# The second exchange of a spectral layer: half of it copied block by block inside SBUF

## The chip, the cores and the metric

The kernel runs on one core of a Trainium2 chip. The metric is the device time of one launch in microseconds (us). TensorE is called PE, VectorE DVE, ScalarE ACT, GpSimd POOL, SyncE SP; the last issues most DMAs. SBUF is the on-chip memory with 128 partitions, PSUM the accumulators' memory, DRAM the memory outside.

## The reference

Four layers on one sequence of 2048 rows by 512 columns, in bfloat16: spectral, attention, spectral, attention, each added to its input. Both kinds start with a layer norm. The spectral layer is a two-dimensional real FFT, a product with a complex weight, and the inverse:

```python
def _A_ref(x, w_r, w_i):
    B, S, D = x.shape
    X = rfft2(x.astype(float32), axes=(-2, -1))
    W = w_r + 1j * w_i
    X = X * W
    return irfft2(X, s=(S, D), axes=(-2, -1)).astype(bfloat16)

x = x + _A_ref(_layernorm(x), A_w_r, A_w_i)
x = x + _B_ref(_layernorm(x), B_wq, B_wk, B_wv, B_wo)
x = x + _A_ref(_layernorm(x), A_w_r, A_w_i)
x = x + _B_ref(_layernorm(x), B_wq, B_wk, B_wv, B_wo)
```

`_B_ref` is attention with 32 query heads of 16 and one shared key and value head. It takes most of the time and is not touched by the change.

## The kernel before, in words

The spectral layer does each FFT as matrix products. The FFT along the 2048 rows is split as 2048 = 128 x 16: a product over 128 points, a twiddle, and a product over 16 points follow one another, and between the products the data must be dealt out anew over the partitions. That is an *exchange*. There are two in a layer: one on the way forward (tiles A1 to A2, through DRAM tensor D1) and one on the way back (tiles B1 to B2, through D2). The 256 complex frequencies along the columns are worked in two halves, `h` = 0 and 1, of 128 each; a tile such as B1 has the shape 128 partitions x 2 halves x 16 blocks x 256 numbers.

The steps around the change are these, by the names in `spectral_layer`:

- `blocks(q)` (L261): POOL builds the block tables H1, H2, H2N and for two of the four `q` H1N, from a table HC and a mask: fourteen products a layer (L266). In the second layer they stand on POOL ahead of the last `ln_rstd` (L163) of the norm, on which the forward product waits.
- `filtered(j)` (L330), j = 0 to 7, four for each half: the 16-point product of four blocks (PE, table G), a copy to X (ACT, L339) and the products with the weights (DVE, L343, L345), for odd j the sums into Z in `joined` (L358, L359).
- `back(j)` (L361): the 16-point inverse of the four blocks `b4` to `b4 + 3`, two blocks at a time: PE products with the H tables, then a copy from PSUM to B1 (L375 on ACT; L373 on DVE for the last pair of all), then one DMA on SP that writes the two blocks to D2 (L376).
- `cross2(h, g, eng)` (L378): one of four reads of D2 to B2 for a half. Each takes four of the 16 values of `t` for all 128 partitions, and needs all sixteen blocks of the half to be in D2. For half 0 all four are on SP; for half 1 two are on SP and two on ACT (L421).
- `along(q, h)` (L396): for two values of `t`, four PE products with lhsT from B2 and the table CS (L401), then a copy to AT on ACT or DVE (L404, L406).
- `last(t, h)` (L410): the product along the columns into a PSUM sum, started with the residual (L414 to L416), after which ACT copies the row tile to x_sb (L435) and DVE takes its statistics (L157).

The order of `filtered`, `back` and the reads of half 0 is written out by hand:

```python
STEPS = "f0 f1 f2 b0 f3 b1 b2 j f4 b3 x0 f5 f6 b4 f7 b5 j7 b6 b7"
```

Here `f` is `filtered`, `b` is `back`, `j` is `joined`, `x0` is the four reads of half 0. So half 0's reads go out behind the last write of b3, while steps 4 to 7 (half 1) are still to be computed. After the steps come the eight `along` of half 0, the four reads of half 1, `weights(20)` (in the first layer: loads of wq and wo on SP), four `last(t, 0)`, and then the loop of `along(q, 1)` and `last`. PE, ACT, DVE and SP run in the order in which the program names the instructions; POOL's order is left to the scheduler. DMAs take their completion semaphores from eight in turn, and a DMA waits for the one that used its semaphore before.

In the partition index m of B1 the value m = 8 t + a belongs to `t` of 16 and `a` of 8, since H's columns stand in that order; in B2 the partition index is 16 a + b, with b the block.

Of the kernel before, what the change touches and what calls it, by code (L numbers as in the profile page):

```python
# [10 lines left out]
ALU = mybir.AluOpType  # L11
P = 128
BF = mybir.dt.bfloat16
# [4 lines left out]
S, D, H, DH = 2048, 512, 32, 16  # L18
# [28 lines left out]
LASTW = 6  # L47
NEGATE = 7
DIRECT = (0, 2, 4, 6)
STEPS = "f0 f1 f2 b0 f3 b1 b2 j f4 b3 x0 f5 f6 b4 f7 b5 j7 b6 b7"  # L50
NORMED, NORMG = (1,), ((3,), (3,), (3,))
OUTK, LATE_AT = 2, 4
TWICE = ((7,), 8)
# [23 lines left out]
def host_tables():  # L77
    import ml_dtypes
    bf = lambda a: np.ascontiguousarray(np.asarray(a, dtype=np.float32).astype(ml_dtypes.bfloat16))
    tabs = {}  # L80
    p = np.arange(P, dtype=np.float64)
    m = np.arange(P, dtype=np.float64)
    t16 = np.arange(16, dtype=np.float64)

    row = (128 * np.arange(4)[None, :, None] + np.arange(P)[:, None, None]).astype(np.float64)
    ff = (np.arange(256)[None, None, :] + 1).astype(np.float64)

    half = 2 * np.pi * np.arange(256) / 512.0
    cos, sin = np.cos(half), np.sin(half)
    cos[128], sin[0] = 0.0, 0.0  # L90
    cos[129:], sin[129:] = -cos[1:128][::-1], sin[1:128][::-1]
    turn = (row * ff).astype(np.int64) % 512
    c, s = np.concatenate([cos, -cos])[turn], -np.concatenate([sin, -sin])[turn]
    tabs["PH"] = bf(np.concatenate([c[..., :128], s[..., :128], c[..., 128:], s[..., 128:]], axis=2))

    ang = 2 * np.pi * (16 * p[:, None, None] + t16[None, :, None]) * m[None, None, :] / 2048.0
    tabs["C1"], tabs["S1"] = bf(np.cos(ang)), bf(np.sin(ang))

    ti, ai = np.divmod(np.arange(P), 8)
    same = (ai[:, None] == ai[None, :]).astype(np.float64)  # L100
    ang = 2 * np.pi * ti[:, None] * ti[None, :] / 16.0
    tabs["G"] = bf(np.stack([same * np.cos(ang), same * np.sin(ang), -same * np.sin(ang)], axis=1))

    b16 = np.arange(16, dtype=np.float64)
    mm = 16 * ai[:, None, None] + b16[None, :, None]
    ang = 2 * np.pi * (ti[:, None, None] * t16[None, None, :] / 16.0 + t16[None, None, :] * mm / 2048.0)
    tabs["HC"] = bf(np.stack([np.cos(ang), np.sin(ang), -np.sin(ang), -np.cos(ang)], axis=1))
    tabs["mask8"] = bf(ai[:, None] == np.arange(8)[None, :])

    ang = 2 * np.pi * m[:, None] * p[None, :] / 128.0  # L110
    tabs["CS"] = bf(np.stack([np.concatenate([np.cos(ang), np.sin(ang)], axis=1),
                              np.concatenate([-np.sin(ang), np.cos(ang)], axis=1)], axis=1))

    frow = (128 * np.arange(2)[None, :, None] + np.arange(P)[:, None, None] + 1).astype(np.float64)
    dd = np.arange(512)[None, None, :].astype(np.float64)
    ang = 2 * np.pi * frow * dd / 512.0
    cf = np.where(frow == 256, 1.0, 2.0) / (S * D)
    tabs["PSC"] = bf(cf * np.cos(ang))
    tabs["PSS"] = bf(-cf * np.sin(ang))
    tabs["ident"] = bf(np.eye(P, dtype=np.float32))  # L120
    tabs["hmask"] = (np.arange(P)[:, None] // DH % 2 == np.arange(2)[None, :]).astype(np.float32)
    return tabs


class Tables:


    def __init__(self, nc):
        self.nc, self.host, self.dram = nc, host_tables(), {}
# [82 lines left out]
def rotate(nc, ps, c, s, sn, re_im, first, begin=True, end=True):  # L212

    nc.tensor.matmul(ps, lhsT=c, rhs=re_im, start=begin, stop=False, skip_group_check=True)  # L214
    nc.tensor.matmul(ps[:, 0:128], lhsT=s, rhs=re_im[:, 128:256], start=False, stop=False, skip_group_check=True)
    nc.tensor.matmul(ps[:, 128:256], lhsT=sn, rhs=re_im[:, 0:128], start=False, stop=end, skip_group_check=True)  # L216


def spectral_layer(nc, tc, tabs, ht, A_w_r, A_w_i, x_sb, bigp, pre, norm, att, feed, weights):
    C1, S1, S1N, PH, ident = (tabs[n] for n in ("C1", "S1", "S1N", "PH", "ident"))  # L220
    with tc.tile_pool(name="workA", bufs=2) as work, tc.tile_pool(name="tabA", bufs=1) as tabA, \
# [31 lines left out]
            weights(k)  # L253

        D1 = dram.tile([2, 16, P, 256], BF, name="D1")
        D2 = dram.tile([2, P, 16, 256], BF, name="D2")
        turned = len(feed.xT)
        xT = feed.xT[0] if turned else bigp.tile([P, NC, 16, P], BF, name="xT", tag="big")
        Pk, A1, A2 = big("Pk"), big("A1"), big("A2")
# [1 line left out]
        def blocks(q):  # L261

            b = slice(4 * q, 4 * q + 4)
            shape = [P, 4, 16, 8]
            for i, H in enumerate([H1[:, b], H2[:, b], H2N[:, b]] + ([H1N[q]] if q in H1N else [])):
                nc.gpsimd.tensor_tensor(out=H.rearrange("p b (t a) -> p b t a", a=8),  # L266
                                        in0=tabs["HC"][:, i, b].unsqueeze(3).to_broadcast(shape),
                                        in1=tabs["mask8"].unsqueeze(1).unsqueeze(1).to_broadcast(shape), op=ALU.mult)

        def forward(k, h):  # L270

# [26 lines left out]
        for k in range(9 + behind):  # L298
# [6 lines left out]
            at = k - behind  # L305
# [21 lines left out]
        Z, B1, B2 = big("Z"), big("B1"), big("B2")  # L327
        M = big("M").rearrange("p h t c -> p (h t c)").rearrange("p (i j b r f) -> p i j b r f", i=2, j=4, b=4, r=2)

        def filtered(j):  # L330

            h, b4 = j // 4, 4 * (j % 4)
            hf = slice(128 * h, 128 * h + 128)
            X = work.tile([P, 4, 2, 128], BF, name="X", tag="X", bufs=3)
            for b in range(b4, b4 + 4, 2):
                ps = bank()
                for i in range(2):
                    rotate(nc, ps[:, i, :], G[:, 0, :], G[:, 1, :], G[:, 2, :], A2[:, h, b + i, :], i == 0)
                nc.scalar.copy(out=X[:, b - b4:b - b4 + 2, :, :], in_=ps.rearrange("p j (r f) -> p j r f", r=2))  # L339
            m1, m2 = (M[:, i, j % 4] for i in range(2))  # L340
            wrb = wr_sb[:, b4:b4 + 4, hf].unsqueeze(2).to_broadcast([P, 4, 2, 128])
            wib = wi_sb[:, b4:b4 + 4, hf].unsqueeze(2).to_broadcast([P, 4, 2, 128])
            nc.vector.tensor_tensor(out=m1, in0=X, in1=wrb, op=ALU.mult)  # L343
            joined()
            nc.vector.tensor_tensor(out=m2, in0=X, in1=wib, op=ALU.mult)  # L345
            if j in DIRECT:
                unsummed[j] = (m1, m2)
            else:
                products.append((j, m1, m2))
# [3 lines left out]
        def joined():  # L353

            while products:
                j, m1, m2 = products.pop()
                Zv = Z[:, j // 4, 4 * (j % 4):4 * (j % 4) + 4, :].rearrange("p b (r f) -> p b r f", r=2)
                nc.vector.tensor_tensor(out=Zv[:, :, 0, :], in0=m1[:, :, 0, :], in1=m2[:, :, 1, :], op=ALU.subtract)  # L358
                nc.vector.tensor_tensor(out=Zv[:, :, 1, :], in0=m1[:, :, 1, :], in1=m2[:, :, 0, :], op=ALU.add)  # L359

        def back(j):  # L361
            h, b4 = j // 4, 4 * (j % 4)
            for b in range(b4, b4 + 4, 2):
                ps = bank()
                for i in range(2):
                    if j in DIRECT:
                        m1, m2 = (m[:, b + i - b4].rearrange("p r f -> p (r f)") for m in unsummed[j])
                        rotate(nc, ps[:, i, :], H1[:, b + i, :], H2N[:, b + i, :], H2[:, b + i, :], m1, i == 0, True, False)
                        rotate(nc, ps[:, i, :], H2N[:, b + i, :], H1N[j % 4][:, b + i - b4, :], H1[:, b + i, :], m2, False, False)
                    else:  # L370
                        rotate(nc, ps[:, i, :], H1[:, b + i, :], H2N[:, b + i, :], H2[:, b + i, :], Z[:, h, b + i, :], i == 0)
                if j == 7 and b > b4:
                    nc.vector.tensor_copy(out=B1[:, h, b:b + 2, :], in_=ps)  # L373
                else:
                    nc.scalar.copy(out=B1[:, h, b:b + 2, :], in_=ps)  # L375
                nc.sync.dma_start(out=D2[h, :, b:b + 2, :], in_=B1[:, h, b:b + 2, :])  # L376

        def cross2(h, g, eng):  # L378
            eng.dma_start(out=B2[:, h, 4 * g:4 * g + 4, :],
                          in_=D2[h].rearrange("(t a) b c -> t (a b) c", t=16)[4 * g:4 * g + 4].rearrange("t m c -> m t c"))  # L380

        for step in STEPS.split():
            j = int(step[1:] or 0)
            if step[0] == "f":
                filtered(j)
            elif step[0] == "b":
                back(j)
            elif step[0] == "j":
                joined()
            else:  # L390
                for g in range(4):
                    cross2(0, g, nc.sync)

        AT = big("AT").rearrange("p h t c -> p (h t c)").rearrange("p (t h c) -> p t h c", t=16, h=2)

# [21 lines left out]

        for q in range(8):
            along(q, 0, q % 2 == 0)
        for g in range(4):  # L420
            cross2(1, g, (nc.sync, nc.scalar)[g % 2])  # L421
        weights(20)
        early = 4
        for t in range(early):
# [2 lines left out]
        for q in range(9):  # L427
# [9 lines left out]
            g, odd = divmod(q - 3, 2)  # L437
# [863 lines left out]
```

## Time and profile before

| what | value |
|---|---|
| median of 3 runs | 1403.78 us (1402.68 to 1403.95) |
| the profiled execution's own time | 1402.49 us |
| its span, from the first to the last instruction | 1400.7 us |
| PE busy | 1348.2 us (96%) |
| ACT busy | 1331.4 us (95%) |
| DVE busy | 1305.8 us (93%) |
| POOL busy | 849.4 us (61%) |
| DMA moved | 32.70 MB |
| D<-B writes, 128 KB each | 32, median 3.0 us from issue to landing |
| B<-D reads, 256 KB each | 12 on SP, 3.9 us; 4 on ACT, 4.4 us |

The profile is of one execution. A row "A<-D" is a DMA or an instruction that writes tile A from tile D; tile names come without numbers, so A is A1 or A2, D is D1 or D2, B is B1 or B2. "SPq" is SP's queue of DMA issues. The first spectral layer lies in the first 80 us of the span, the second between about 705 and 790 us; the rest is attention, in which ACT, PE and DVE are all nearly full. The high shares of the whole page are those of attention. The change lies in the spectral layers, so they are read by themselves.

### The profile page before, as it was taken

To read this page: it belongs to the slowest core of one execution; us is meant where nothing else is said; L and a number is where in the kernel's file an instruction comes from. 1 tells how busy PE (TensorE), PEld (TensorE's weight loads), DVE (VectorE), ACT (ScalarE), POOL (GpSimd) and SP (SyncE) were. 2 spreads that over 40 slices of the span, in tenths; PEclk is the share of its full clock that TensorE was granted. 3 is DMA by queue.
4 is the path that set the end of the run, shared out by engine and by line. 5 is a ranking of instruction groups with operands and counts; after the bars stand their busy time and mean duration, and the time that the engine had idled before them with its cause. 6 is when DMAs were issued, how large, how long until landed. Compare 5 with 4: busy or idle time off the path is not lost.

```text
span 1400.7 us, 35023 instructions
## 1 busy us (share of the span) xinstructions
PE 1348.2 (96%) x14146; PEld 477.7 (34%) x14214; DVE 1305.8 (93%) x2253; ACT 1331.4 (95%) x1542; POOL 849.4 (61%) x507
## 2 busy tenths in 40 slices
PE   7899999999999999999999999999999999999998
PEld 6752232222222222222277422322223222222222
DVE  5689999999999999999966899999999999999997
ACT  6679999999999999999957899999999999999997
POOL 3325666667666667666640367666667667666664
PEclk9999999999999999999999999999999999999999
DMA  8700000000000000002064000000000000000000
GB/s 243 209 17 2 1 2 2 2 2 2 2 1 1 2 2 2 2 1 37 11 166 137 2 2 2 2 1 9 5 6 2 6 9 5 2 6 5 9 2 16
DMA packets 45395, 32.70 MB, mean 23 GB/s; under 512 B 10160, under 2 KB 43184, under 8 KB 44720
## 3 DMA queue, kind: packets, MB, share of 16 engines
q1 hardware_dynamic: 42832, 29.24, 7.4%
q8 instruction: 111, 1.82, 0.5%
q10 hardware_dynamic: 2400, 1.21, 0.3%
q14 instruction: 52, 0.43, 0.1%
HBM read 18.39 MB, written 10.49 MB: 21 GB/s over the span
## 4 chain that ended last, share of the span: by engine, by line
ACT 48%; PE 33%; issue 9%; DVE 6%; DMA 2%; POOL 1%; SPq 0%; DVEq 0%; ACTq 0%; POOLq 0%
ACT e L1099 47%; PE pv L888 13%; PE sc L933 10%; DVE ph L973 3%; PE aux L933 2%; PE ps L214 1%; PE ps L275 1%; DVE ln_stats L157 1%; PE aux L472 1%; DMA B<-D 1%; DVE ph L1005 1%; PE pv L903 1%; PE aux L701 1%; POOL tab_H L266 1%; PE ps L216 1%
## 5 line engine op out<-in xcount | busy, mean ns | idle before, releaser
L1099 ACT ACTIVATE e<-sc 128x1024 bf16<-128x1024 f32 x1328 | 1218.1, 1163 | 2.9 <-PE sc L933 2.9
L997 POOL TENSOR_TENSOR ph<-ph,step 128x1024 int32<-128x1024 int32 x404 | 763.3, 1893 | 412.3 <-DVE ph L1005 291.8
L973 DVE TENSOR_SCALAR ph<-aux 128x512 uint16<-128x512 f32 x1440 | 904.0, 679 | 20.4 <-PE aux L933 15.8
L888 PE MATMUL pv<-ph,vaug 128*32 128x512 bf16 x4320 | 548.8, 386 | 0.6 <-POOL ph L997 0.3
L933 PE MATMUL sc<-QT,Kv 32*128 32x512 bf16 x2656 | 521.9, 380 | 23.2 <-ACT e L1099 15.9
L888 PE MATMUL pv<-e,vaug 128*32 128x512 bf16 x2656 | 484.0, 384 | 0.3 <-ACT e L1099 0.3
L933 PE MATMUL aux<-QT,Kv 32*128 32x512 bf16 x1440 | 456.0, 384 | 1.0 <-DVE ph L973 0.5
L933 PEld LDWEIGHTS <-Kv 32*128 32x128 bf16 x4096 | 183.2, 91 | 525.5 <-issue 517.2
L903 PE MATMUL pv<-wo_sb,zeros 128*32 128x512 bf16 x1200 | 257.9, 383 | 0.0
L888 PEld LDWEIGHTS <-vaug 128*32 128x32 bf16 x6976 | 147.7, 94 | 293.0 <-issue 282.0
L1005 DVE TENSOR_SCALAR ph<-ph 128x2048 uint16<-128x2048 uint16 x316 | 216.6, 685 | 0.5
L163 POOL TENSOR_TENSOR ln_rstd<-ln_veps,mhalf 128x4 f32<-128x4 f32 x16 | 16.5, 1034 | 107.2 <-DVE ln_veps L162 107.1
L157 DVE BATCH_NORM_STATS2 ln_stats<-x_sb 128x6 f32<-128x512 bf16 x64 | 43.5, 679 | 23.3 <-ACT x_sb L435 17.2
L903 PEld LDWEIGHTS <-zeros 128*32 128x32 bf16 x1200 | 60.1, 94 | 1.9 <-issue 0.3
L803 DVE STREAM_TRANSPOSE oT<-pv 128x512 f32<-128x512 f32 x64 | 45.3, 707 | 9.2 <-PE pv L888 9.2
L186 ACT ACTIVATE Pk<-ps,ln_rstd 128x256 bf16<-128x256 f32 x64 | 26.7, 473 | 21.0 <-PE ps L275 16.1
L289 DVE CAST A<-ps 128x512 bf16<-128x512 f32 x28 | 19.2, 689 | 19.8 <-PE ps L216 18.7
L275 PE MATMUL ps<-tab_PH,xT 128*128 128x256 bf16 x256 | 35.6, 288 | 1.7 <-DMA tab_PH<-const_PH 0.8
L472 PE MATMUL aux<-xTa,wq_sb 128*128 128x512 bf16 x90 | 32.6, 385 | 2.8 <-issue 2.4
L825 POOL TENSOR_TENSOR on<-oT,rden 128x512 bf16<-128x512 f32 x30 | 31.7, 1058 | 2.0 <-DVE rden L829 1.8
L701 PE MATMUL aux<-wo_sb,ph 128*128 128x512 bf16 x72 | 26.1, 383 | 3.6 <-issue 2.1
L275 PEld LDWEIGHTS <-xT 128*128 128x128 bf16 x256 | 25.4, 103 | 6.0 <-issue 1.5
(117 smaller groups left out, 715.2 us busy)
## 6 DMA issues: line engine op xcount, KB each, us to landing
D<-A SPq DMA_DIRECT2D x32, 128.0 KB, 2.7
A<-D SPq DMA_DIRECT2D x16, 256.0 KB, 3.3
D<-B SPq DMA_DIRECT2D x32, 128.0 KB, 3.0
B<-D SPq DMA_DIRECT2D x12, 256.0 KB, 3.9
wr_sb<-in_A_w_r_dram SPq DMA_DIRECT2D x2, 1024.0 KB, 7.0
wi_sb<-in_A_w_i_dram SPq DMA_DIRECT2D x2, 1024.0 KB, 8.9
out_dram<-x_sb SPq DMA_DIRECT2D x15, 128.0 KB, 1.7
x_sb<-in_A_x_dram SPq DMA_DIRECT2D x3, 512.0 KB, 8.2
```

What stands on the lines that cost most here:

```text
L157: nc.vector.bn_stats(st, src)
L275: nc.tensor.matmul(ps[:, j, :], lhsT=xT[:, cc, 2 * k + j, :], rhs=PH[:, cc, 256 * h:256 * h + 256], start=(cc == 0), stop=(cc == NC - 1), ...
L472: self.nc.tensor.matmul(ps, lhsT=w(c), rhs=self.xTq[:, c, qc * 512:(qc + 1) * 512], start=(c == 0), stop=(c == NC - 1), skip_group_check=True)
L701: nc.tensor.matmul(ps, lhsT=OTs[qb][:, g4, kk * P:(kk + 1) * P], rhs=wo_sb[:, g4, :], start=first, stop=last, skip_group_check=True)
L803: end = clock.now(clock.FLIP, lambda: nc.vector.transpose(out=oT[:, par].rearrange("p b c -> p (b c)"), in_=pv), clock.last + clock.MM_END)
L888: nc.tensor.matmul(pv_tiles[gi][32 * i:32 * i + 32, :], lhsT=vaug[:, kc, j, :], rhs=es, start=((gi, i) not in started), stop=(left[gi, i] ...
L903: nc.tensor.matmul(pv_tiles[gi][32 * i:32 * i + 32, :], lhsT=att.zeros, rhs=wo_sb[:, 0, :], start=False, stop=False, skip_group_check=True)
L933: nc.tensor.matmul(out, lhsT=Kv[r, par, kc * P:(kc + 1) * P], rhs=QT[r, g, qb * 512:(qb + 1) * 512], start=True, stop=True, skip_group_che ...
L973: end = clock.now(clock.Z, lambda: nc.vector.tensor_scalar(out=z.bitcast(U16), in0=ps, scalar1=SCALE * LOG2E * 128.0, scalar2=127.0 * 128. ...
L997: nc.gpsimd.tensor_tensor(out=copy.bitcast(I32), in0=z.bitcast(I32), in1=step.to_broadcast([P, w // 2]), op=ALU.add)
L1005: nc.vector.tensor_scalar(out=one.bitcast(U16), in0=z.bitcast(U16), scalar1=float(PHASE[1]), scalar2=None, op0=ALU.add)
L1099: nc.scalar.activation(out=e[:, 0:ng * 512], in_=sc[:, 0:ng, :].rearrange("p a b -> p (a b)"), func=ACT.Exp, scale=SCALE)
```

## The change

The four `back` steps of half 1 (j = 4 to 7) no longer write D2. After each pair of blocks, two DMAs on SP copy the blocks straight from B1 to B2, one block per DMA: 128 source partitions of 512 B each go into eight destination partitions of 8 KB each, four partitions apart. So half 1 has sixteen copies of 64 KB and no reads. The four steps of half 0 still write D2 and read it back, but each read now belongs to one `back` step: it takes the four blocks of step g and fills 32 partitions with 8 KB each.

For this the order of partitions is changed on both sides. H's columns, and so the partitions of B1, become m = 16 a + t, so that the sixteen `t` of one `a` stand side by side; B2's partition becomes 32 g + 4 a + b', where b' is the block within step g, and the rows of the table CS are put into that order on the host. The tables H are computed with their two inner axes exchanged. The products on PE keep their number and shapes.

```diff
-STEPS = "f0 f1 f2 b0 f3 b1 b2 j f4 b3 x0 f5 f6 b4 f7 b5 j7 b6 b7"
+STEPS = "f0 f1 f2 b0 f3 b1 b2 j f4 b3 x0 x1 x2 x3 f5 f6 b4 f7 b5 j7 b6 b7"
...
     tabs["CS"] = bf(np.stack([np.concatenate([np.cos(ang), np.sin(ang)], axis=1),
-                              np.concatenate([-np.sin(ang), np.cos(ang)], axis=1)], axis=1))
+                              np.concatenate([-np.sin(ang), np.cos(ang)], axis=1)], axis=1)[16 * (np.arange(P) // 4 % 8) + 4 * (np.arange(P) // 32) + np.arange(P) % 4])
...
-        D2 = dram.tile([2, P, 16, 256], BF, name="D2")
+        D2 = dram.tile([2, 4, 4, P, 256], BF, name="D2")
...
-            shape = [P, 4, 16, 8]
+            shape = [P, 4, 8, 16]
             for i, H in enumerate([H1[:, b], H2[:, b], H2N[:, b]] + ([H1N[q]] if q in H1N else [])):
-                nc.gpsimd.tensor_tensor(out=H.rearrange("p b (t a) -> p b t a", a=8),
-                                        in0=tabs["HC"][:, i, b].unsqueeze(3).to_broadcast(shape),
-                                        in1=tabs["mask8"].unsqueeze(1).unsqueeze(1).to_broadcast(shape), op=ALU.mult)
+                nc.gpsimd.tensor_tensor(out=H.rearrange("p b (a t) -> p b a t", a=8),
+                                        in0=tabs["HC"][:, i, b].unsqueeze(2).to_broadcast(shape),
+                                        in1=tabs["mask8"].unsqueeze(1).unsqueeze(3).to_broadcast(shape), op=ALU.mult)
...
-                nc.sync.dma_start(out=D2[h, :, b:b + 2, :], in_=B1[:, h, b:b + 2, :])
+                if j >= 4:
+                    for bb in (b, b + 1):
+                        at = 32 * (j % 4) + bb - b4
+                        nc.sync.dma_start(out=B2[at:at + 29:4, h, :, :], in_=B1[:, h, bb, :])
+                else:
+                    nc.sync.dma_start(out=D2[h, j % 4, b - b4:b - b4 + 2].rearrange("b p c -> p b c"), in_=B1[:, h, b:b + 2, :])
 
-        def cross2(h, g, eng):
-            eng.dma_start(out=B2[:, h, 4 * g:4 * g + 4, :],
-                          in_=D2[h].rearrange("(t a) b c -> t (a b) c", t=16)[4 * g:4 * g + 4].rearrange("t m c -> m t c"))
+        def cross2(h, g):
+            nc.sync.dma_start(out=B2[32 * g:32 * g + 32, h, :, :],
+                              in_=D2[h, g].rearrange("b (a t) c -> a b (t c)", t=16))
...
             else:
-                for g in range(4):
-                    cross2(0, g, nc.sync)
+                cross2(j // 4, j % 4)
...
         for q in range(8):
             along(q, 0, q % 2 == 0)
-        for g in range(4):
-            cross2(1, g, (nc.sync, nc.scalar)[g % 2])
         weights(20)
```

## The prediction

> **What bounds the kernel now.** I read the page first (span, shares, the chain of work that ended last), then that chain in order of time around the second exchange of each spectral layer, then PE's timeline there, then what the DMA queues move, and POOL's groups.
>
> ```profile
> span 1400.7 us, 35023 instructions
> ACT 48%; PE 33%; issue 9%; DVE 6%; DMA 2%; POOL 1%; SPq 0%; DVEq 0%; ACTq 0%; POOLq 0%
> ```
> DMA holds 2% of the chain: exchanges end last at only a few places. Here is the chain in order of time in the first spectral layer, then in the second (start, length, what):
>
> ```profile
> 60.70 2.93 DMA D<-B
> 63.76 3.35 DMA B<-D
> 67.16 0.62 PE ps L401 x4
> ...
> 752.65 2.99 DMA D<-B
> 755.76 3.32 DMA B<-D
> 759.12 0.62 PE ps L401 x4
> ```
> The last block of the second half is written to DRAM (2.9 us) and read back (3.3 us), and only then does `along` (L401) go on. PE's timeline says how much of these 6.3 us nobody covers (in brackets: idle before, and who ended it):
>
> ```profile
> 67.16 1.05 PE L401 MATMUL ps<-tab_CS,B 128*128 128x256 bf16 x8 [1.43 <-DMA B<-D]
> ...
> 759.12 0.61 PE L401 MATMUL ps<-tab_CS,B 128*128 128x256 bf16 x4 [1.46 <-DMA B<-D]
> ```
> So PE is ready at 65.73 and 757.66, and all that a shorter second exchange can give is 1.43 + 1.46 = 2.89 us, 0.21% of the time. I take 0.2% (2.8 us) as about what a measurement of this kernel tells from no change. Behind the idle time the chain runs through L401, the sums and the statistics on DVE without slack, so a microsecond there is a microsecond of the end.
>
> **The SP queue and the DMA engines.** One line is one run of issues; then stretches of the busy table (last columns: granted clock, DMA share, GB/s) and one queue's share of the stretch 757.90 to 760.40.
>
> ```profile
> 54.55 2.50 SPq L379 DMA_DIRECT2D B<-D  x4
> 57.09 4.01 SPq L376 DMA_DIRECT2D D<-B  x8
> ...
> 755.80:756.80 1.00, 1.00 (x6) 0.47 (x5) 0.01 (x1) 0.00 (x0) 0.00 (x0) 1.00 0.00 0
> 737.75:738.50 0.75, 0.75 (x13) 0.69 (x10) 0.75 (x4) 0.69 (x2) 0.00 (x0) 1.00 0.72 218
> 757.90:760.40 2.50, 1.05 (x8) 0.70 (x8) 0.00 (x0) 0.63 (x2) 0.00 (x0) 1.00 1.16 319
> ...
> q1 hardware_dynamic: 711, 0.35, 49.2%
> ```
> Eight issues fill 4.01 us: 0.50 us each. The read issued at 755.76 moves nothing until 756.80: 1.04 us to the first packet. Reads into 128 partitions (B<-D, 757.90) run at 319 GB/s, a read into 32 partitions (A<-D, 737.75) at 218. In the last line (same 2.5 us stretch) 711 packets of 512 B take 49.2% of 16 engines: 0.492 x 16 x 2500 / 711 = 28 ns a packet.
>
> **The change, part by part.**
>
> *First half (h=0).* Eight D2 writes keep their number and place; their runs fall from 1 KB to 512 B. The nearest row is D<-A, same shape, median 2.7 us to landing against 3.0 for D<-B: nothing. The four reads now land in 32 partitions each, in 8 KB runs, as A<-D does, and the first `along` waits for all four instead of one. SP reaches them where it did: after the last write of b3, issued 52.46 to 52.78 and 744.05 to 744.50, so at about 52.88 and 744.60. With 1.04 us to the first packet, data starts at 53.92 and 745.64. A 256 KB read at A<-D's 218 GB/s takes 1.20 us; four take 4.8 (at least 3.3, at B<-D's rate). They end at 58.72 and 750.44. PE wants them at 59.4 and 751.4 (first L401), so this stays hidden, by 0.4 us in the first layer with a tail of 0.25.
>
> *Second half (h=1): what goes.* Eight writes and four reads per layer, two of the reads on ACT's queue (1.00 us of issue at 63.77; ACT is idle there from 63.32 to 67.80, so its relief is worth nothing), and the write-then-read wait.
>
> *What comes.* Sixteen copies of 64 KB, all on SP, 128 packets of 512 B each into 8 partitions. SP issue: 16 x 0.50 = 8.0 us from about 55.0, instead of 4.0: the last goes out at 62.5 (first layer; the last B1 tile is ready at 60.37). With a first packet 1.04 us later that is 63.5, not yet the limit; at the longest issue among B<-D's rows (0.97 us) it would go out at 69.6. Behind the copies on SP stand the wq and wo loads (landed 70.86 and 72.31, first used at about 81): still early enough. The program has eight DMA semaphores in turn, so the eighth copy waits for the last read to land (about 750.7) and the ninth for the first copy; at 0.50 us an issue this also ends before the data does.
>
> *The data of a copy* is the price no row shows. From below: 64 KB at 319 GB/s, 0.21 us. From above: if the rate shrinks with the destination partitions from 32 to 8, 218/4 = 55 GB/s, 1.2 us. Going from 128 to 32 partitions cost a factor 319/218 = 1.46; another such step gives 149 GB/s, 0.44 us. Eight rows written side by side, 16 packets of 28 ns each, give 0.45 us. I take 0.45. The copies queue behind the four reads: 16 x 0.45 = 7.2 us. First layer: 53.92 + 4.8 + 7.2 + 0.25 (from the last packet to the semaphore, an estimate: under 0.1 to about 0.5 in the rows) = 66.17, against 65.73: PE idles 0.44 + 0.05 instead of 1.43, gain 0.94. Second layer: 745.64 + 4.8 + 7.2 + 0.25 = 757.89, against 757.66: 0.28 instead of 1.46, gain 1.18. Together 2.1 us.
>
> *H tables on POOL.* The same fourteen products a layer, with the repeated operand changed. This matters in the second layer, where they stand in the chain ahead of the normalisation:
>
> ```profile
> L266 POOL TENSOR_TENSOR tab_H1N<-tab_HC,tab_mask 128x512 bf16<-128x512 bf16 x4 | 4.2, 1038 | 0.0
> L825 POOL TENSOR_TENSOR on<-oT,rden 128x512 bf16<-128x512 f32 x30 | 31.7, 1058 | 2.0 <-DVE rden L829 1.8
> ```
> L825 already repeats one operand along its innermost 16 elements, as the new form does, and takes 1058 ns: at most 0.02 us more, over 14 chained products 0.28; nothing excludes as much less. I take 0, because the element count is the same. The reordered CS table and the reordered partitions of B2 leave `along` with the same shapes; PE, DVE and POOL keep their order.
>
> **Sum.** The profiled execution took 1402.49 us (span 1400.7 and 1.8 around it). 1402.49 - 2.1 = 1400.4. The median of the runs, 1403.78, is 1.29 above that execution, so I give 1401.7, 0.15% less.
>
> **Rivals.**
>
> *A, wholly hidden.* If copies take up to 0.42 us, the last lands before PE needs it and the gain is 2.89: 1399.6 against the profiled execution, 1400.9 on the median. For it: packets of both sides spread over 16 engines would give 0.22 us. Against it: the rate already falls from 319 to 218 with fewer partitions. [...]
>
> *B, the other side: the copies become the bound.* Place: the DMA queue between the last read and the last copy. It decides from 16 t = 67.11 - 53.92 - 5.05, t = 0.51 us a copy (0.52 in the second layer): above that the copies land later than today's read, and each further 0.1 us costs 1.6 us a layer. At 0.65 us PE goes on 2.26 and 2.01 us later than now: 1402.49 + 4.3 = 1406.8, 1408.1 on the median; from 0.61 it is over 0.2%. For it: the fall of the rate with fewer partitions, and that no row has both sides in SBUF. Against it: 28 ns packets with eight rows abreast give 0.45. [...]
>
> *C, the first `along` waits.* If four reads take over 5.2 us they delay PE at 59.4, but PE then also needs the copies later; it costs only what it adds to the copies' end, 0.1 to 0.5 us, and is part of the forecast's own spread.
>
> *D, POOL.* The new table form costs 0.2 us a product more: 14 x 0.2 = 2.8, 1404.5 on the median after the gain. No row speaks for so much.
>
> **Chances.** Forecast, partly hidden (0.42 to 0.52 us a copy): 0.42. A: 0.17. B: 0.36, of it 0.26 beyond 0.61 us. D and the unforeseen: 0.05. Faster by over 0.2%: three quarters of A, which lies on the edge, a tenth of the forecast's cases, 0.01 of the rest: 0.18. Slower: 0.26 of B and 0.04 of the rest: 0.30. Within: 0.52. The range runs from A, with 0.7 for the scatter of the runs, 1400.2, to just past B at 0.65, 1408.5; what lies beyond is the far end of 1.2 us a copy (16 x 0.75 us more a layer, 1425 or so) and luck. The likeliest case alone: 1400.9 to 1403.8.
>
> **What would show it.** PE's idle time before the first L401 of the second half: 0.2 to 0.7 us if right, 0 for A, over 1.5 for B. Time between landings of successive copies when queued: 0.45 us. Reads of the first half: about 1.2 us apart, the last landed by 59.2 and 751.0. L266 at 1.04 us. SP at 0.50 us an issue. Wrong would be: copies slower than 0.51 us, SP issues near 1 us, or an idle PE at 59.4 of over half a microsecond.

## The result, and the profile after

| | median | range | runs |
|---|---|---|---|
| before, beside it | 1404.51 us | 1402.68 to 1406.21 | 8 |
| after | 1408.37 us | 1405.83 to 1410.85 | 8 |

The ratio is 1.0029, with an interval of 1.0018 to 1.0041: the change costs 0.29%, about 4 us, where 2.1 us of gain were forecast. The time lies at the upper end of the range, close to the 1408.1 that rival B gave. That agreement is luck: B gave it for copies 0.65 us apart, and for the 0.70 to 0.73 us that were measured B's own sum gives about 1410.

The page of the profile after, its first line and the shares of the chain of work that ended last:

```profile
span 1408.8 us, 35032 instructions
ACT 49%; PE 32%; issue 9%; DVE 7%; POOL 1%; DMA 1%; SPq 0%; DVEq 0%; ACTq 0%; POOLq 0%
```

The span is 8.1 us longer than that of before in this execution (1410.54 us against a median of 1408.37). DMA's share of the chain has fallen from 2% to 1%, which says nothing about the time; PE's timeline does. These are the first `along` products (L405 here) of half 0 in the first layer, then of half 0 and half 1 in the second, with the idle time before them in brackets:

```profile
63.27 1.04 PE L405 MATMUL ps<-tab_CS,B 128*128 128x256 bf16 x6 [1.78 <-DMA B<-B]
...
757.66 0.60 PE L405 MATMUL ps<-tab_CS,B 128*128 128x256 bf16 x4 [1.94 <-DMA B<-D]
...
765.50 0.93 PE L405 MATMUL ps<-tab_CS,B 128*128 128x256 bf16 x7 [1.59 <-DMA B<-B]
```

Before, PE waited only ahead of half 1, 1.43 and 1.46 us (1.59 and 1.94, 1.42 and 1.83 in two further profiles of that kernel). Now it waits 1.78 and 1.94 us ahead of half 0, where it had not waited at all, and in the second layer 1.59 us ahead of half 1 as well. (The first row names a copy, though half 0 uses no copied block; a second profile of the same kernel names the read there.) The sum over both layers has gone from 2.89 to 5.31 us. In the first layer half 1 doesn't wait only because PE is late by then.

SP's issues show why. First layer, then second; start, length, number:

```profile
54.81 3.10 SPq L384 DMA_DIRECT2D B<-D  x4
57.96 11.14 SPq L379 DMA_DIRECT2D B<-B  x16
...
748.90 3.05 SPq L384 DMA_DIRECT2D B<-D  x4
752.00 11.62 SPq L379 DMA_DIRECT2D B<-B  x16
```

Four reads hold SP for 3.1 us, 0.76 each, and sixteen copies for 11.6, 0.73 each. The forecast had 0.50. SP goes from one copy to the next almost without a pause: the instruction alone lasts 0.61 (minimum, median and maximum, in ns):

```profile
L379 SPq DMA_DIRECT2D B<-B x16: 608/608/650, 752.0 to 763.0; - x16
...
L384 SPq DMA_DIRECT2D B<-D x8: 643/667/823, 54.8 to 751.3; - x8
```

The chain in order of time has both in it, in the second layer (start, length, what):

```profile
749.13 0.53 SPq L384
749.76 0.70 SPq L384
750.55 0.64 SPq L384
751.31 6.22 DMA B<-D
...
761.64 0.61 SPq L379
762.35 0.61 SPq L379
763.01 2.25 DMA B<-B
```

The fourth read needs 6.22 us from its issue until its data is there, 0.14 us ahead of PE's start. What the DMA engines do meanwhile is in the table of stretches (last columns: granted clock, DMA share, GB/s). Its last row is the stretch behind the wait ahead of half 1:

```profile
753.00:757.20 4.20, 2.68 (x35) 2.21 (x32) 2.26 (x5) 2.28 (x5) 0.00 (x0) 1.00 0.49 163
757.20:764.90 7.70, 6.19 (x43) 4.24 (x44) 2.77 (x4) 2.34 (x4) 0.00 (x0) 1.00 0.51 137
...
766.90:770.30 3.40, 3.40 (x11) 1.51 (x10) 1.70 (x4) 2.06 (x4) 0.00 (x0) 0.50 0.00 0
```

While only reads run the sixteen engines are half busy (0.49) and move 163 GB/s, as if eight of them worked. The four reads' packets run from 750.44 to 757.20, 6.8 us, or 1.69 us a read. The outermost size of these reads in DRAM is 8; in the run with flat reads below it is 32, and the share is 0.99. The forecast reckoned with eight rows side by side for the copies and not for the reads.

The last row shows PE at half its clock (0.50) for 3.4 us after the wait. In that time it does 1.7 us less work, an estimate from the 3.4 us and the 0.50. Such a stretch stands three times in the spectral layers of this profile (46.7, 63.7, 766.9) and not once in that of before; a second profile of before has one, from 68.6 us, behind its wait of 1.59. The granted clock over the whole run tells how many there were: the runs of after had 0.996 to 1.000, and so had those of before (a stretch of 3.4 us at half clock takes 0.0012 off). At a clock of 1.000, 20 runs of before (from three of the comparisons below, on other chips) have a mean of 1402.7 us and 2 of after 1406.3; at 0.996, 6 of before have 1406.9 and 4 of after 1409.5. At equal clock the change thus costs about 2.6 to 3.6 us, and in the medians of all runs 3.9.

The tables cost what was forecast. The block tables on POOL in the second layer take a median of 1035 ns against 1037 before:

```profile
L266 POOL TENSOR_TENSOR tab_H<-tab_HC,tab_mask x8: 1033/1035/1255, 709.1 to 721.3; 128x512 bf16<-128x512 bf16 x8
```

The attention layers are the same (607.4 us from the first to the last exponential of the second one, in both). So the difference lies in the spectral layers: in these two profiles the first exponential of the first attention layer comes 3.88 us later (97.10 against 93.22), and the second spectral layer takes 83.46 us instead of 79.58 from its first product to the first exponential, 3.88 us more. In the second layer the waits explain 2.07 us of it (1.94 + 1.59 - 1.46) and the half-clock stretch about 1.7. In the first they have grown by 0.35 us only (1.78 against 1.43); more of the loss stands there beside two half-clock stretches and an idle time near 46 us, ahead of the second exchange, which is taken up near the end of the experiments.

### The profile page after: what moved, and what is told of

It is laid out like the page before. It is cut to its first block, busy times and chain, and to the rows that moved or that the text cites. A ratio compares the mean times of both kernels' runs of the same rounds, so it can differ in the third digit from the quotient of the medians.

```text
span 1408.8 us, 35032 instructions
## 1 busy us (share of the span) xinstructions
PE 1350.4 (96%) x14146; PEld 478.2 (34%) x14214; DVE 1307.1 (93%) x2253; ACT 1331.4 (95%) x1542; POOL 849.7 (60%) x507
## 4 chain that ended last, share of the span: by engine, by line
ACT 49%; PE 32%; issue 9%; DVE 7%; POOL 1%; DMA 1%; SPq 0%; DVEq 0%; ACTq 0%; POOLq 0%
ACT e L1101 48%; PE pv L890 12%; PE sc L935 10%; DVE ph L975 3%; PE aux L935 2%; PE ps L214 1%; DVE ln_stats L157 1%; PE ps L275 1%; PE ps L405 1%; DVE ph L1007 1%; PE aux L474 1%; PE ps L420 1%; PE ps L419 1%; PE pv L905 1%; PE aux L703 1%
## 5 line engine op out<-in xcount | busy, mean ns | idle before, releaser
L408 ACT CAST AT<-ps 128x512 bf16<-128x512 f32 x24 | 14.0, 592 | 15.8 <-PE ps L405 13.6
```

## The experiments

All times are medians beside runs of the kernel before on the same chip. Of each edit the lines that matter are shown, against the changed kernel.

### The two halves of the change, each alone

**Half 0 alone.** Half 1 keeps the DMAs of before, in a DRAM tensor of its own.

```diff
-                    for bb in (b, b + 1):
-                        at = 32 * (j % 4) + bb - b4
-                        nc.sync.dma_start(out=B2[at:at + 29:4, h, :, :], in_=B1[:, h, bb, :])
+                    nc.sync.dma_start(out=D2o[:, b:b + 2, :], in_=B1[:, h, b:b + 2, :])
```

> Only the first half's part of the change is kept; the second half's DMAs have the old shapes and places (their values come out permuted, so the result is not the reference's). Theory 1 (two new bounds: the four reads of 8 KB runs land late, and SP's issue of the copies is slow): PE idles 1.5 to 2.2 us ahead of the first product of half 0 in each layer, and 1.4 to 1.5 us ahead of half 1 as before the change; with one or two half-clock windows of 1.7 us behind those waits the time is 3 to 7 us over the kernel before. Theory 2 (only the copies cost): within 1 us of the kernel before, no wait ahead of half 0.

1409.01 us, ratio 1.0036 [1.0023, 1.0048]. PE waits 2.18 and 2.48 us ahead of half 0. Ahead of half 1 it doesn't wait in the second layer, where the late start covers the old round trip through DRAM, but 1.86 us in the first, where it doesn't. A half-clock stretch follows each wait ahead of half 0, and none the third wait. The reads of half 0 alone cost as much as the whole change.

**Copies alone.** Half 0 keeps the writes and reads of before.

```diff
-                cross2(j // 4, j % 4)
+                cross2old(0, j, nc.sync)
```

> Only the copies of the second half are kept; the first half's DMAs have the old shapes (its values come out permuted). Theory 1: no wait ahead of half 0; SP issues a copy each 0.66 us, 16 x 0.66 = 10.6 us from about 57.1 in the first layer, so the last lands near 69.5 and PE idles 2.5 to 4 us ahead of half 1 instead of 1.4: 2 to 5 us over the kernel before, plus half-clock windows. Rival (the data of the copies bounds, 0.5 us or more each): copies queue up, landings 0.5 us apart behind an SP that is ahead. Rival (only the reads cost): 1.5 to 2.9 us under the kernel before.

1411.55 us, ratio 1.0047 [1.0034, 1.0061]. Half 0 is on time, and half 1 comes later than with the round trip that the copies replace: PE waits 4.29 and 3.73 us instead of 1.43 and 1.46, and the loss is 6.8 us where 2 to 5 were expected. The waits of PE in the second layer, then SP's issues there:

```profile
PE ps L406 <- DMA B<-B: 3.7, 1, 3.7
```

```profile
751.21 2.02 SPq L385 DMA_DIRECT2D B<-D2o  x4
753.27 11.35 SPq L379 DMA_DIRECT2D B<-B  x16
```

Each half by itself is as bad as both, and in the changed kernel they partly hide each other: half 0's late start gives the copies time.

### What makes the copies slow

**Straight copies.** Each copy goes from 128 partitions to 128 partitions.

```diff
-                        at = 32 * (j % 4) + bb - b4
-                        nc.sync.dma_start(out=B2[at:at + 29:4, h, :, :], in_=B1[:, h, bb, :])
+                        nc.sync.dma_start(out=B2[:, h, 15 - bb, :], in_=B1[:, h, bb, :])
```

> The changed kernel, but each of the 16 copies goes from 128 partitions to the same 128 partitions (same 64 KB in 128 packets of 512 B, same order; the values land in wrong places). Theory 1 (a DMA with 8 rows outermost is slow to issue): an issue takes 0.32 to 0.45 us instead of 0.61, no wait is left ahead of half 1, the wait of 1.8 us ahead of half 0 stays: 1.5 to 3.5 us under the changed kernel. Rival (any SBUF to SBUF copy is slow to issue): issue stays at 0.61 and the time within 0.7 us of the changed kernel.

1408.45 us, ratio 1.0027 [1.0017, 1.0037], no better. Copies over 128 rows on both sides also hold SP, if a little less:

```profile
L378 SPq DMA_DIRECT2D B<-B x16: 465/569/1230, 752.0 to 762.9; - x16
```

Sixteen of them last until 763.5 as well, and in the second layer PE still waits 1.42 us ahead of half 1, against 1.59. The eight rows thus are not what makes a copy dear to issue; they account for some 0.04 (median) to 0.14 us (minimum) of 0.61.

**Two queues, with half 0's reads split.** Every second copy goes out on POOL's queue; half 0's first two reads are issued before b3. It was run beside the same order on SP alone.

```diff
-STEPS = "f0 f1 f2 b0 f3 b1 b2 j f4 b3 x0 x1 x2 x3 f5 f6 b4 f7 b5 j7 b6 b7"
+STEPS = "f0 f1 f2 b0 f3 b1 b2 x0 x1 j f4 b3 x2 x3 f5 f6 b4 f7 b5 j7 b6 b7"
...
-                        nc.sync.dma_start(out=B2[at:at + 29:4, h, :, :], in_=B1[:, h, bb, :])
+                        (nc.sync, nc.gpsimd)[bb % 2].dma_start(out=B2[at:at + 29:4, h, :, :], in_=B1[:, h, bb, :])
```

> The changed kernel with the four reads of half 0 issued earlier on SP (two behind b2, two behind b3); nothing else. Theory 1 (late reads plus copies bound by SP's issue): no wait ahead of half 0; the first copy is issued about 1 us earlier, and 16 of them at 0.66 us still end late: PE idles 1.7 to 2.5 us ahead of half 1. 1 to 3.5 us under the changed kernel, 0.5 to 3 us over the kernel before. Rival (the reads alone cost): under the kernel before by 1.5 to 2.9 us. Rival (what costs lies outside both exchanges): as the changed kernel.

> As the last one, but every second copy is issued from POOL, which is idle there, so SP issues 8 copies instead of 16. If SP's issue bounds the copies (theory 1): SP is through at about 61.5 in the first layer, the wait ahead of half 1 falls under 0.5 us, and the time is 1.5 to 3 us under the kernel before, unless POOL takes over 1.2 us for a copy of its own, when POOL is the new bound. If the eight rows in SBUF or the DMA engines bound them: the wait ahead of half 1 stays at 1.7 us or more.

Early reads alone: 1413.05 us, ratio 1.0058 [1.0044, 1.0071]. SP's issues in the second layer:

```profile
742.54 4.87 SPq L381 DMA_DIRECT2D D<-B  x6
747.58 1.55 SPq L384 DMA_DIRECT2D B<-D  x2
749.17 0.95 SPq L381 DMA_DIRECT2D D<-B  x2
750.22 4.26 SPq L384 DMA_DIRECT2D B<-D  x2
754.53 11.44 SPq L379 DMA_DIRECT2D B<-B  x16
```

The two early reads stand in front of b3's writes; the last read then waits on SP for those writes, and all copies wait behind it. They start at 754.53 instead of 752.00, and half 1 waits 3.57 us. Half 0, for which no wait was expected, waits 2.56 and 1.42 us. My theory that an earlier issue is an earlier landing was wrong here.

With the second queue: 1407.40 us, ratio 1.0024 [1.0013, 1.0035], over the kernel before and not 1.5 to 3 us under it. The wait ahead of half 1 is gone in both layers, though the copies start as late. Eight copies on SP now take 6.04 us:

```profile
754.65 6.04 SPq L379 DMA_DIRECT2D B<-B  x8
```

So the copies were bound by SP's issue and not by their data. Half 0 still waits, 3.48 and 1.86 us.

**Second queue alone.** The changed kernel, with only the line of the copies from above.

> The changed kernel with every second copy issued on POOL's queue, everything else as it is. Theory (the copies are bound by SP's issue): the idle ahead of half 1 falls from 1.59 to 0 in the second layer; in the first it was 0 because the first along was late; half 0's wait stays 1.5 to 2 us: 1406 to 1408. Rival (they are bound by the data): the wait stays and so does the time, 1408 to 1409.

1407.87 us, ratio 1.0026 [1.0017, 1.0036]. In the second layer half 1 waits about 0.1 us instead of 1.59 and half 0 still 1.72; in the first 0 and 2.94. The one wait of the L405 products in the second layer that the table of waits lists (us in all, times, longest):

```profile
PE ps L405 <- DMA B<-D: 1.7, 1, 1.7
```

The reading holds and the gain is small: the waits ahead of half 0 are left, and the one in the first layer is longer in this profile than in that of after.

### What makes half 0 late

**Flat reads.** Half 0's read takes 32 rows of 8 KB in one run of DRAM.

```diff
-                              in_=D2[h, g].rearrange("b (a t) c -> a b (t c)", t=16))
+                              in_=D2[h, g].rearrange("b (a t) c -> (b a) t c", t=16))
```

> The changed kernel, with half 0's four reads taken as 32 rows of 8 KB in one run of DRAM instead of 8 by 4 by 8 KB; the rows of half 0 come to other partitions, so the values are another order's. Theory (the shape, outermost 8, puts a read on eight engines with a long issue): SP issue per read falls from 0.65 to 0.8 to below 0.5 us, the four land at least 1 us sooner, the idle ahead of half 0 falls from 1.94 to below 1 us in the second layer; about 2 us over the two layers: 1405 to 1407.5. Rival (the wait is the round trip through DRAM of the last write and is not the shape's): the idle ahead of half 0 stays at 1.5 to 2 us and the time at 1408 to 1409.

1406.18 us, ratio 1.0012 [1.0003, 1.0021]. The same bytes to the same partitions (in another order): issue falls from 667 to 376 ns, all sixteen engines are busy (0.99, 226 GB/s, against 0.49 and 163), and half 0's wait in the second layer falls from 1.94 to 0.19 us, which is a wait for ACT and no longer for a DMA. The read's row, a stretch with reads alone, and the first product of half 0:

```profile
L384 SPq DMA_DIRECT2D B<-D x8: 303/376/418, 52.9 to 748.0; - x8
```

```profile
747.60:752.00 4.40, 4.37 (x60) 3.98 (x58) 4.19 (x9) 3.83 (x8) 0.00 (x0) 1.00 0.99 226
```

```profile
753.54 0.49 PE L405 MATMUL ps<-tab_CS,B 128*128 128x256 bf16 x3 [0.19 <-ACT B L375]
```

The four reads' packets now last 5.1 us instead of 6.8, and the forecast had 4.8. In the second layer it is the read's shape that makes half 0 late, and the edit takes away about 2 us of the change's cost. In the first layer 1.33 us are left; there the reads' packets run until 60.2, with packets of copies between the last of them, and no run here says why. Half 1, whose copies are still on one queue, waits 1.57 and 1.75 us.

**Flat reads and two queues.** Both edits.

> Both edits: flat reads for half 0 (values in another order) and every second copy on POOL's queue. Theory: both waits are small in both layers, 1402.5 to 1405.5, at or under before. Rival (the waits only hide a loss elsewhere): 1407 or over with no wait ahead of either half.

1405.03 us, ratio 1.0004 [0.9995, 1.0014]: the time of before. In the second layer the waits are 0.41 and 0.42 us; in the first 1.67 and 1.20 are left. Undoing the two causes undoes the loss, to within the interval, but doesn't bring the gain.

### The half clock

**PE kept busy.** Matmuls without use run in the two waits, eight and seven of them.

```diff
+        def warm(n):
+            ps = psum.tile([P, 512], F32, name="ps", tag="pa")
+            for _ in range(n):
+                nc.tensor.matmul(ps, lhsT=ident, rhs=PSC[:, 0, :], start=True, stop=True, skip_group_check=True)
+
+        warm(8)
         for q in range(8):
             along(q, 0, q % 2 == 0)
...
+            if q == 0:
+                warm(7)
```

> The changed kernel with 8 and 7 idle products on PE (1.7 and 1.5 us) in its two waits, ahead of half 0 and of half 1. Theory 3 (the waits set off half-clock windows of 3.4 us, each worth 1.7 us): no half clock in the spectral layers behind the two waits, 1.5 to 3.5 us under the changed kernel on the median. Against it: the same time or up to 0.7 us more, half clock as before.

1408.44 us, ratio 1.0029 [1.0018, 1.0041]: no better. The clock does stay up behind the waits, at 64 and at 766.9, and a stretch before them remains:

```profile
47.30:50.70 3.40, 3.40 (x28) 2.91 (x26) 1.98 (x5) 1.75 (x3) 1.01 (x6) 0.50 0.92 233
64.00:67.40 3.40, 3.40 (x33) 3.05 (x32) 2.08 (x3) 2.09 (x4) 0.00 (x0) 1.00 0.52 143
766.90:770.30 3.40, 3.16 (x21) 1.74 (x19) 1.48 (x4) 3.19 (x7) 0.00 (x0) 1.00 0.00 0
```

In this profile the second layer is 1.45 us shorter than in the changed kernel's (82.01 against 83.46 us from its first product to the first exponential), which answers to one stretch. With no half clock left it is still 2.43 us longer than that of before (79.58), so half clock is not the whole loss there. What it is worth in the first layer this run can't tell: the seven products, 1.5 us, stand there too, where the changed kernel had no wait ahead of half 1, and can hide what the clock gains.

### Less copied, and more

**Last step only.** Only the blocks of b7 are copied; b4 to b6 go through DRAM, read on POOL's queue; half 0's first two reads early as above.

```diff
-STEPS = "f0 f1 f2 b0 f3 b1 b2 j f4 b3 x0 x1 x2 x3 f5 f6 b4 f7 b5 j7 b6 b7"
+STEPS = "f0 f1 f2 b0 f3 b1 b2 x0 x1 j f4 b3 x2 x3 f5 f6 b4 f7 b5 x4 j7 b6 x5 b7 x6"
...
-                if j >= 4:
+                if j >= 7:
...
-            nc.sync.dma_start(out=B2[32 * g:32 * g + 32, h, :, :],
+            (nc.sync, nc.gpsimd)[h].dma_start(out=B2[32 * g:32 * g + 32, h, :, :],
```

> Early reads for half 0; in half 1 only the last back step is copied inside SBUF (4 copies on SP), steps 4 to 6 go through DRAM like those of half 0, with their reads issued from POOL. Theory 1: SP has 6 writes of 0.5 us and 4 copies of 0.66 us instead of 16 copies, the last copy is issued by about 63.0 in the first layer and PE idles under 0.8 us ahead of half 1: 1 to 2.9 us under the kernel before. Rival (a copy is slow however few there are): wait of 1.4 us or more, within 1 us of the kernel before.

1413.71 us, ratio 1.0059 [1.0043, 1.0075]. The mixed order has half 0's late reads (waits of 4.10 and 1.65 us) and three more of the same kind, with waits of 3.73 and 0.92 us ahead of half 1. The gain of 1 to 2.9 us that was expected did not come, and what four copies alone would bring is not shown.

**All copied, two queues.** No write to DRAM and no read at all; 32 copies a layer, even blocks on SP, odd ones on POOL.

```diff
-STEPS = "f0 f1 f2 b0 f3 b1 b2 j f4 b3 x0 x1 x2 x3 f5 f6 b4 f7 b5 j7 b6 b7"
+STEPS = "f0 f1 f2 b0 f3 b1 b2 j f4 b3 f5 f6 b4 f7 b5 j7 b6 b7"
...
-                if j >= 4:
+                if j >= 0:
...
-                        nc.sync.dma_start(out=B2[at:at + 29:4, h, :, :], in_=B1[:, h, bb, :])
+                        (nc.sync, nc.gpsimd)[bb % 2].dma_start(out=B2[at:at + 29:4, h, :, :], in_=B1[:, h, bb, :])
```

> All eight back steps are copied block by block, even blocks on SP's queue and odd ones on POOL's; there is no write to DRAM and no read. Theory (the loss is the reads of half 0, landing 1.8 to 1.9 us late, and the issue of the copies on one queue, 0.61 us each): b3's copies are issued some 7 us before the first along, so both waits go in both layers (after: 1.78 and 1.94 ahead of half 0, 0 and 1.59 ahead of half 1), and the half clock behind them; the time is that of before less its own two waits, 1.43 and 1.46, up to 2.9 us under it: 1401.5 to 1404.5, ratio 0.998 to 1.000. Rival (the copies load something that the spectral layers need, whatever is waited for: twice as many would cost more): 1409 or over, ratio above 1.003. Rival (the loss sits in the early part of the first layer, ahead of the exchange): the waits go and the time stays at 1406 to 1408.

1400.35 us, ratio 0.9971 [0.9960, 0.9981]: faster than both kernels, and under the 1401.5 to 1404.5 that were expected. The first products of half 1 in the first layer, and of both halves in the second:

```profile
66.98 0.49 PE L405 MATMUL ps<-tab_CS,B 128*128 128x256 bf16 x3 [1.28 <-DMA wq_sb<-in_B_wq_dram]
...
751.51 0.60 PE L405 MATMUL ps<-tab_CS,B 128*128 128x256 bf16 x4
...
757.60 0.49 PE L405 MATMUL ps<-tab_CS,B 128*128 128x256 bf16 x3
```

The second layer has no wait left, and from its first product to the first exponential it takes 77.93 us against 79.58 before: 1.65 us, the wait of 1.46 and a little. In the first layer half 1 still waits 1.28 us. The row names the load of wq; POOL's last copy lands at 66.25, shortly before, and which of the two it waited for isn't settled. At a granted clock of 1.000 this kernel's three runs have a mean of 1400.1 us, 2.7 under the mean of before on the same chip (1402.8, 11 runs); the medians differ by 3.9. Half-clock stretches in the runs of before don't account for the rest: at a clock of 0.998 the means differ by 4.46 us (1400.18 of 3 runs against 1404.64 of 10). So the gain is shown, and what makes the part of it beyond the waits is open.

**All copied, one queue.** The same with all 32 copies on SP.

> All eight back steps copied block by block, all 32 copies of a layer on SP's queue. Theory (half 0's reads and SP's issue are the two causes): no wait ahead of half 0, since the copies of b0 to b3 go out as the blocks come; ahead of half 1 about 0 to 1.6 us as in the changed kernel, SP holding 0.61 to 0.66 us a copy and no reads (3.0 us of issue) ahead of half 1's copies, so rather 0 to 0.7: 1401 to 1403.5, a little behind the kernel with two queues (1400.4). Rival (the second queue was what helped): 1405 or over.

1413.46 us, ratio 1.0063 [1.0048, 1.0078]: among the slowest here, where 1401 to 1403.5 was expected. PE waits 1.15 and 4.85 us in the first layer, and 4.35 ahead of half 1 in the second. SP's row and PE's:

```profile
744.90 22.37 SPq L379 DMA_DIRECT2D B<-B  x32
```

```profile
769.22 0.38 PE L405 MATMUL ps<-tab_CS,B 128*128 128x256 bf16 x2 [4.35 <-DMA B<-B]
```

32 copies take 22.37 us, 0.70 each, almost without a gap: this layer goes at the pace of SP's issues alone. I had thought of half 0's copies as going out while its blocks are computed, and so as free. They hold SP for 11 us, longer than eight writes (0.36 to 0.45 each) and four reads (0.76) do, and half 1's copies stand behind them. With two queues the copies begin as early, counted from the layer's first product (31.9 us after it, here 32.1), and SP has issued its sixteen in 15.6 us. Copying everything is a gain only with a second queue.

### The two kernels once more

**Before, beside itself.** No edit.

> The kernel before, profiled once more. It tells whether what the changed kernel shows early in the first layer (POOL's H tables beside DVE's products until 45.8 us, PE idle for 2.5 us near 47, a half-clock window there) belongs to the change. If it does not: the same start here, with PE idle for 1.6 us or more near 46 and the first product of half 0 up to 2 us later than the 59.48 of the first profile. If it does: as the first profile, idle for 0.8 us. The waits ahead of half 1 are 1.4 to 1.5 us either way.

1404.66 us, ratio 0.9999 [0.9989, 1.0009], so 0.1% is what such a comparison tells apart. PE is idle for 0.82 us near 46, as in the first profile. **A second profile of after and a third of before:**

> The changed kernel once more, for a second profile of it. If the longer idle near 47 us of the first layer (2.51 us, against 0.82 before) is scatter of the input's arrival, it may come out at 0.82 or 1.67 here; if it belongs to the change it is 2.51 again. The waits ahead of half 0 (1.8 to 1.9) and half 1 (0 and 1.6) come again either way.

> The kernel before once more, for a third profile. If the idle near 46 us is scatter it may come out at 1.67 or 2.51; if it belongs to the kernel it is 0.82 a third time. The waits ahead of half 1, 1.4 to 1.9, come again.

In the second profile of after (1410.03 us) the waits come again, 2.40 and 0 us in the first layer, 1.61 and 1.78 in the second. One more difference lies earlier, near 46 us of the first layer. PE's row there before and after:

```profile
46.70 0.27 PE L214 MATMUL ps<-Z,tab_H 128*128 128x256 bf16 x1 [0.82 <-ACT X L339]
```

```profile
47.15 0.37 PE L214 MATMUL ps<-Z,tab_H 128*128 128x256 bf16 x1 [2.51 <-DVE Z L359]
```

PE is idle there for 2.51 us in both profiles of after, and for 0.82, 0.82 and 1.67 us in three of before; the longer times are waits for DVE's sums (L359). DVE's products there take 1.52 us instead of 0.68 while POOL builds its tables, and the more of them fall into that time the longer PE waits. In all seventeen profiles the idle time follows one interval, from POOL's first table product, which waits for the mask to be loaded, to DVE's first product (L343): where that is 10.93 us or more it is 0.82, from 9.97 to 10.88 it is 1.67, at 9.70 or less it is 2.51. Before had 11.41, 10.93 and 10.67, after 9.70 and 9.55, and the variants lie anywhere from 9.03 to 11.61. In before and after no transfer of the second exchange has been issued by then, and both kernels that copy everything, which have the tables of after, show 0.82. So the new tables alone don't do it. Whether the rest of the change has a part in the order of arrival stays open; it is worth up to 1.7 us in one execution, and it may be in the difference of the medians.

## Why the prediction was wrong, point by point

Two steps of it failed: the reads of half 0, which were to stay hidden, and the issue of the copies on SP, which was to end before their data.

- **The bound** (2.89 us of idle time ahead of half 1 is all there is to win): not refuted, but not shown either. With everything copied and two queues the second layer gains 1.65 us where the wait was 1.46, and the runs at full clock gain 2.7 in all; their medians differ by 3.9, and two further profiles of before have 3.53 and 3.25 us of such idle time instead of 2.89.
- **Half 0, "so this stays hidden, by 0.4 us":** wrong, and the main error. Two terms of the step were mis-sized. First packet after 1.04 us: 1.54 (748.90 to 750.44). "A 256 KB read at A<-D's 218 GB/s takes 1.20 us; four take 4.8": 1.69 each, 6.8 in all. That is 0.5 + 2.0 = 2.5 us later than reckoned; the second layer's slack was 751.42 - 750.44 - 0.25 = 0.73 (first product of half 0 before, the forecast's end of the reads, its tail), so a wait of 1.8 follows, and it is 1.94. The sign of being wrong that the forecast had named, PE idle ahead of half 0 for over half a microsecond, is there in both layers. The A<-D row has 0.72 of sixteen engines busy, more than eight, and was not the near row that I took it for: its size in SBUF is alike, but its outermost size in DRAM is 32 and not 8. Flat reads, with 0.99 of sixteen engines busy, take 5.1 us and bring the wait to 0.19. All this is the second layer; in the first the cause of what flat reads leave, 1.33 us, is open.
- **SP's issue, "SP issue: 16 x 0.50 = 8.0 us", "at 0.50 us an issue this also ends before the data does":** wrong. 16 copies take 11.1 and 11.6 us of SP, and this sets the end of half 1: with half of the copies on a second queue its wait in the second layer falls from 1.59 to about 0.1 us. I had taken the price from the writes to DRAM (D<-B, eight in 4.01 us), although the four reads in the same fence took 2.50 us, 0.63 each, and B<-D's longest, 0.97 us, was in the text as the far end; the range's upper part I had left to the data.
- **The data of a copy, 0.45 us:** too high. Where copies queue up behind the reads (from 757.2) they follow each other by 0.38 us (933 packets of 512 B, or 7.3 copies, in 2.8 us). So rival A's condition, up to 0.42 us a copy, was met and its gain still did not come. No run shows a copy's data at 0.61 us or more, to which the forecast gave a chance of 0.26, nor at the 0.65 of the range's upper end; measured were the 0.38. The error in the data did not matter, since the copies are spaced by SP, 0.70 to 0.73 us apart. (That no row has both sides in SBUF was not quite so: the page of before has twelve transposes xT<-x_sb; none is a plain copy.)
- **Rival C, "it costs only what it adds to the copies' end, 0.1 to 0.5 us":** this was the right mechanism with a price about four times its upper end. The wait was held to be absorbed because the copies would end later anyway. In the first layer the late half 0 did absorb the wait ahead of half 1, but it was itself longer than that wait; in the second, both were paid.
- **Rival B (the copies become the bound):** it named the right side, but not the place. The bound lies in SP's issue, ahead of the DMA queue that B spoke of.
- **H tables, nothing:** right, 1035 ns against 1037.
- **Left out: the half clock.** In the profile of after a stretch of 3.4 us at half clock goes with each of the waits of 2.51, 1.78 and 1.59 us, and none with that of 1.94. The half clock was in no term of the sum. It lengthens a single run (by about 1.7 us a stretch, the estimate from above); in the second layer the run that keeps PE busy shows 2.43 us of loss without it.
- **Left out: the idle time near 46 us of the first layer.** It is 0.84 to 1.69 us longer in the profiles of after than in those of before. Whether the change makes it longer is not known, so the share of the waits in the first layer's loss is argued and not shown.

## What to carry to other kernels

A DMA's price had three parts here: the issue on its queue (0.61 us for a copy), the delay to the first packet (1.54 for a read), and the data (1.69 for a read); look which of them spaces the transfers before pricing the one that is easiest to compute. Take each from a row with the same shape on both sides, outermost size above all (a read with 8 took 667 ns to issue at a DMA share of 0.49, with 32 it took 376 at 0.99), and if no row has that shape, let the far end of each term into the sum: here the issue of a copy was wrong by 0.2 us, times 16, and the data of a read by 0.5 us, times 4. When a consumer that took its input piece by piece comes to need all of it at once, look for its new wait first; and when a gain is worth at most one short wait, it may pay to try the change whole (here, all copied, with the issues shared by two queues) before a half of it that keeps both prices.

## What was not expected of the hardware

- Issuing a copy inside SBUF held SP for a median of 0.61 us (eight destination rows) or 0.57 (128 rows); a read from DRAM held it for 0.38 where the DMA share was 0.99, and for 0.67 where it was 0.49. With both queues in use, in the kernel that copies everything, the same copy took 0.61 on SP and 0.59 on POOL:

```profile
L379 SPq DMA_DIRECT2D B<-B x16: 613/614/696, 737.7 to 752.6; - x16
L379 POOL DMA_DIRECT2D B<-B x16: 594/594/682, 738.2 to 752.7; - x16
```

- The 32 copies inside SBUF that stood in a row on one queue went at the pace of the issue: 0.70 us each, with 64 KB each, 94 GB/s.
- A wait of PE of 1.6 us was followed by 3.4 us at half clock, in a layer where PE is otherwise nearly full (84.95 of 90 us from 700 to 790 in the profile of before). The wait of 1.94 us just before it was not followed by one, so the length alone doesn't settle it.
